# Staggering the row merges of gathered expert units against their high and low halves

## The chip, the core and the metric

One core of one Trainium2 chip runs the kernel. The metric is device time in microseconds, the median of several executions. Engines are named as in the profile: PE is TensorE (PEld its weight loads), DVE is VectorE, ACT is ScalarE, POOL is GpSimd, SP is SyncE, which issues most DMAs here (SPq is its queue).

## What is computed

Three stages in a row over 4608 tokens of width 512: linear attention with an RMS norm, a dense layer with a maximum of three products, and a top-2 mixture of eight experts. The change lies in the last stage alone:

```python
noisy_logits = x @ w_gate + np.log1p(np.exp(x @ w_noise)) * noise
top2 = np.argpartition(-noisy_logits, 2, axis=1)[:, :2]
# top2_w: softmax over the two chosen logits
for e in range(8):
    for k in range(2):
        mask = top2[:, k] == e
        h = np.maximum(x[mask] @ w1[e], 0.0)        # 512 -> 1024
        out[mask] += top2_w[mask, k, None] * (h @ w2[e])   # 1024 -> 512
```

## The kernel before

**Numbers in two halves.** Matrix products run on float32 values split into a high half (rounded to the fast matmul type) and a low half (the rest). A product is three passes: high by high, high by low, low by high. The split of a weight block is `split` (L292 on ScalarE for the high half, L293 on VectorE for the low half).

**Rows by expert.** While the dense layer runs in nine chunks of 512 tokens, each token's row is scattered to a table `Xg` in device memory, sorted by expert. A row is stored as two planes of 16 bits. The mixture then works on **units**: a unit is one, two or four blocks of 128 rows of one expert, with that expert's weights. The order is fixed: units 0, 1 and 2 have four blocks, and from unit 3 on a four-block unit (odd numbers) is followed by a small one (even numbers): units 4, 6 and 8 have one block, units 10 to 24 have two. Five spare one-block units stand behind branches that are not taken here.

**A unit's steps.** A unit has eight steps, f = 0 to 7, one for each 128 columns of the hidden width. Step f does the first product of f (`G1`, L1068; for a one-block unit L1082, at even f only, two f at once), then ScalarE's Relu (L1072 or L1085) and VectorE's low half (L1073). For a one-block unit the result is transposed two steps later (`hT1`, L1093, with L1094 and L1095 for its halves h). The second products (`G2`, L1130) of a step wait in a list `fifo`, sorted by unit and f, until a step number given with them: for larger units two steps later; for a one-block unit two steps after `hT1` for its first f and three for its second. At f = 7 ScalarE scales the output row out of its PSUM bank (L1135) and POOL adds it to the output by an indirect DMA (L1104). Four PSUM banks serve the second products in turn (`abank`), four the first products and transposes (`hbank`).

**Preparing the next unit.** During unit u the rows of unit u + 1 are made ready by `utrans`, block by block. The two 16-bit planes come by a transposing DMA into RA or RB (`load_rows`, L755, with weights and tokens of the rows at L756). A block is then *merged*: two copies (L790) interleave the planes into one of two buffers MG, one copy on VectorE and the other on ScalarE, or both on VectorE where `tight` is set (while a one-block unit runs). Then ScalarE makes the high half (L793) and VectorE the low half (L794) in the unit's x, which all first products of unit u + 1 read. Before, one call does all four instructions of a block. For u > 1 blocks 0 and 1 are called in step 2 and blocks 2 and 3 in step 4; for u < 2 in steps 3 and 5.

**Queues.** Every engine runs its instructions in the order in which this code writes them; a waiting instruction holds all behind it. SP's queue holds the register loads for a unit's expert and start row (`regs_of`, L741 and L742), the row DMAs and the weight loads (`load_pair`, L144) into three staging buffers. A load is written when the second split of the block three before it is. Before, unit u asks for the rows of unit u + 2 in step 4 if unit u + 1 has four blocks, otherwise in step 2. The table `SPL` says how many weight splits are written in each step:

```python
    SPL = {4: (2,) * 8, 2: (1,) * 8, 1: (0, 0, 0, 0, 0, 0, 1, 1)}
```

A split is left out when its weight slot may still be read or its load is not written yet. Within a step the order is: first product, transposes (`turn`), second products (`flush`), a piece of the table of units (steps 0 to 9 only), then `utrans` and `splits`.

Of the kernel before, what the change touches and what calls it, by code (L numbers as in the profile page):

```python
# [12 lines left out]
U16 = mybir.dt.uint16  # L13
# [72 lines left out]
def body(tc, A, dbg=None):  # L86
# [695 lines left out]

    def utrans(u, i, tight=False):
        s = slice(i * 128, (i + 1) * 128)
        pl = rplanes(u)
        g = MG[mgn[0] % 2]
        mgn[0] += 1
        h = g.bitcast(U16).rearrange("p (k t z) -> p k t z", k=4, z=2)
        for q in range(2):
            (ACT.copy if q and not tight else DVE.tensor_copy)(h[:, :, :, q], pl[:, 4 * q:4 * q + 4, s])  # L790
        t = g.rearrange("p (k t) -> p k t", k=4)
        x = xTu[u % 2]
        ACT.activation(x[0][:, :, s], t, AF.Copy)  # L793
        DVE.tensor_tensor(x[1][:, :, s], t, x[0][:, :, s].bitcast(F), op=OP.subtract)  # L794
        if i == units[u] - 1:
            m = units[u]
            DVE.tensor_copy(wid[u % 3][:, 0:m], gt[u % 3][:, 0:m, 0])
            DVE.tensor_copy(idt[u % 3][:, 0:m], gt[u % 3][:, 0:m, 1])


    def splits(k):
# [68 lines left out]
    def window(c):  # L870
# [8 lines left out]
        def trans(i):  # L879
            xtrans(c + 1, i) if nx else utrans(0, i)  # L880

# [7 lines left out]
        for i in range(4):  # L889
# [10 lines left out]
            if not nx:  # L900
                if i < 2:
                    trans(2 * i)
                    trans(2 * i + 1)
                if i == 1:
                    load_rows(1)
                splits(1)
# [181 lines left out]
    def hT1(u, f, hr):  # L1088
# [7 lines left out]
        fifo.append((step[0] + 2, u, f, h, 0))  # L1096
        fifo.append((step[0] + 3, u, f + 1, h, 128))

# [73 lines left out]
    tg = table()  # L1172
    SPL = {4: (2,) * 8, 2: (1,) * 8, 1: (0, 0, 0, 0, 0, 0, 1, 1)}

    def unit(u):
        mn = units[u + 1] if u + 1 < len(units) else 0
        for f in range(8):
            G1(u, f)
            turn(step[0])
            flush(step[0])  # L1180
            for _ in range(pump.get(step[0], 0)):
                next(tg, None)
            if u < 2:
                if f in (3, 5):
                    for i in range(2):
                        utrans(u + 1, f - 3 + i)
                if u == 1 and f == 7:
                    load_rows(3)
            splits(SPL[units[u]][f])
            if u > 1:  # L1190
                if f in (2, 4):
                    for i in range(f - 2, min(f, mn)):
                        utrans(u + 1, i, units[u] == 1)
                if f == (4 if mn == 4 else 2) and u + 2 < len(units):
                    regs_of(u + 2)
                    load_rows(u + 2)
                    loads()
            step[0] += 1
# [61 lines left out]
```

## Time and profile before

| what | value |
|---|---|
| median of 3 runs | 1556.95 us (1556.66 to 1558.84) |
| the profiled execution's own time | 1555.75 us |
| its span, first to last instruction | 1554.0 us |
| PE busy | 1515.0 us, 97% |
| DVE, ACT, POOL busy | 51%, 42%, 14% |
| mean granted clock of PE | 0.991 of full |
| mixture stage | from some 702 us to the end |

Busy shares are over the whole span. The chain of waits says which engine's work ended last at each moment; the list of waits says who stood for whom. A matmul's shown duration overlaps with the next one's, so the time of a product is read from the chain, which gives the twelve matmuls of a product as one piece.

### The profile page before, as it was taken

The page shows a single profiled execution, that of the slowest core. Times are in us where ns is not written, and L with a number is a line of the kernel's source. Part 1 is how long each engine was busy: PE and PEld are TensorE (multiplying, and loading weights), DVE is VectorE, ACT ScalarE, POOL GpSimd, SP SyncE. Part 2 cuts the span into 40 slices and gives each one's busy share as a digit, 9 for nine tenths or more (in the row PEclk, how much of TensorE's full clock was granted, in tenths as well). Part 3 has the DMA queues.
Part 4 walks back from the last instruction along what each step waited for, and adds up shares of the span by engine and source line. Part 5 has one row for each costly group of instructions (what it writes and reads, how often), then busy time and mean ns, then how long its engine had stood idle before and what let it go on. Part 6 is the DMA issues. An engine that isn't in the chain of part 4 may idle for free.

```text
span 1554.0 us, 23767 instructions
## 1 busy us (share of the span) xinstructions
PE 1515.0 (97%) x9564; PEld 1306.2 (84%) x9564; DVE 792.4 (51%) x1573; ACT 646.0 (42%) x1036; POOL 221.4 (14%) x326
## 2 busy tenths in 40 slices
PE   5999999999999999999999999999999999999997
PEld 4789989898989898888888787778888888888886
DVE  5985534343534343457454456465463554535443
ACT  3544322231313131343454445455464554645544
POOL 0000211111020202024211102101021010211102
PEclk8999999999999999999999999999999999999999
DMA  7322643031212101063676477766695666858554
GB/s 295 134 82 90 254 197 116 29 117 42 103 56 89 56 29 56 1 191 123 205 196 143 109 223 184 169 209 171 162 222 132 196 161 165 202 150 217 148 157 77
DMA packets 132292, 219.82 MB, mean 141 GB/s; under 512 B 96464, under 2 KB 96720, under 8 KB 114640
## 3 DMA queue, kind: packets, MB, share of 16 engines
q1 hardware_dynamic: 112320, 166.50, 34.0%
q0 software_dynamic: 19856, 51.73, 14.7%
q8 instruction: 77, 1.26, 0.3%
q14 instruction: 39, 0.32, 0.1%
HBM read 146.30 MB, written 51.72 MB: 127 GB/s over the span
## 4 chain that ended last, share of the span: by engine, by line
PE 92%; DVE 3%; ACT 2%; DMA 1%; issue 1%; POOL 1%; SPq 0%; POOLq 0%; ACTq 0%
PE bank L311 28%; PE bank L1068 24%; PE bank L1130 24%; PE bank L357 10%; PE bank L192 1%; PE bank L214 1%; PE bank L273 1%; DVE mg L790 1%; ACT B L793 1%; DMA pad<-kvr 1%; PE bank L1082 1%; DMA G<-kv 0%; POOL Xg L427 0%; DVE xlo L794 0%; PE bank L501 0%
## 5 line engine op out<-in xcount | busy, mean ns | idle before, releaser
L311 PE MATMUL bank<-B,W 128*128 128x512 f32 (+1 forms) x2160 | 455.5, 372 | 6.6 <-ACT W L482 4.2
L311 PEld LDWEIGHTS bank<-B,W 128*128 128x128 f32 x2160 | 377.6, 190 | 75.8 <-ACT W L482 4.9
L1130 PE MATMUL bank<-W,B 128*128 128x512 f32 x1728 | 423.3, 392 | 2.0 <-ACT xn L1135 1.9
L1130 PEld LDWEIGHTS bank<-W,B 128*128 128x128 f32 x1728 | 321.2, 189 | 67.0 <-ACT xn L1135 2.3
L1068 PE MATMUL bank<-B,W 128*128 128x512 f32 (+1 forms) x1728 | 355.0, 343 | 6.9 <-ACT B L793 6.9
L1068 PEld LDWEIGHTS bank<-B,W 128*128 128x128 f32 x1728 | 280.9, 190 | 51.1 <-ACT B L793 8.7
L293 DVE TENSOR_TENSOR W<-G,W 128x1024 fp32r<-128x1024 f32 x200 | 242.1, 1223 | 120.2 <-ACT W L292 119.6
L292 ACT ACTIVATE W<-G 128x1024 fp32r<-128x1024 f32 x200 | 207.6, 1055 | 53.3 <-PE bank L1130 39.8
L1073 DVE SCALAR_TENSOR_TENSOR B<-bank,B 128x512 fp32r<-128x512 f32 (+1 forms) x176 | 103.8, 592 | 207.1 <-ACT B L1072 206.6
L1072 ACT ACTIVATE B<-bank 128x512 fp32r<-128x512 f32 (+1 forms) x176 | 90.4, 516 | 266.7 <-PE bank L1068 265.5
L357 PE MATMUL bank<-W,B 128*128 128x256 f32 (+1 forms) x1296 | 164.0, 286 | 0.0
L357 PEld LDWEIGHTS bank<-W,B 128*128 128x128 f32 x1296 | 160.2, 188 | 1.1
L427 POOL DMA_INDIRECT Xg<-RA,si x72 | 72.1, 1001 | 522.1 <-issue 378.1
L329 DVE TENSOR_TENSOR hm<-hm,bank 128x512 f32<-128x512 f32 (+1 forms) x106 | 69.5, 656 | 132.3 <-PE bank L311 125.6
L315 ACT ACTIVATE B<-hm 128x512 fp32r<-128x512 f32 (+1 forms) x53 | 32.2, 607 | 184.7 <-DVE hm L329 184.7
L1068 PE MATMUL bank<-xlo,W 128*128 128x512 f32 x384 | 103.2, 391 | 0.0
L1104 POOL DMA_INDIRECT out<-xn,idt x37 | 61.3, 1655 | 275.3 <-ACT xn L1135 268.3
L1068 PEld LDWEIGHTS bank<-xlo,W 128*128 128x128 f32 x384 | 72.3, 188 | 15.1
L793 ACT ACTIVATE B<-mg 128x512 fp32r<-128x512 f32 x76 | 48.0, 632 | 84.4 <-DVE mg L790 84.3
L1104 POOL DMA_INDIRECT out<-x2T,idt x19 | 30.4, 1602 | 266.0 <-ACT x2T L1135 263.6
L364 ACT COPY RA<-bank 128x256 uint16<-128x256 uint16 x72 | 25.7, 372 | 88.0 <-DVE RA L364 72.7
L794 DVE TENSOR_TENSOR xlo<-mg,B 128x512 fp32r<-128x512 f32 x49 | 34.0, 694 | 36.7 <-ACT B L793 36.7
(184 smaller groups left out, 1010.4 us busy)
## 6 DMA issues: line engine op xcount, KB each, us to landing
G<-mw SPq DMA_DIRECT2D x100, 1024.0 KB, 5.1
G<-w1s SPq DMA_DIRECT2D x12, 1024.0 KB, 4.9
out<-pad POOLq DMA_DIRECT2D x1, 9472.0 KB
kv<-kv SPq DMA_DIRECT2D x8, 1024.0 KB, 7.2
G<-kv SPq DMA_DIRECT2D x8, 1024.0 KB, 9.7
RB<-qT SPq DMA_DIRECT2D x8, 1024.0 KB, 5.1
G<-kvr SPq DMA_DIRECT2D x7, 256.0 KB, 9.8
Xg<-RA,si POOLq DMA_INDIRECT x72, 2.7
```

Source lines behind the costliest of these rows:

```text
L292: ACT.activation(w[:, 0:1024], src, AF.Copy)
L293: DVE.tensor_tensor(w[:, 1024:2048], src, w[:, 0:1024].bitcast(F), op=OP.subtract)
L311: PE.matmul(bank[:, 0:t1 - t0], w_in(g)[:, a, k, s], x[b][:, k, t0:t1], start=n == 0 and k == 0, stop=n == 2 and k == 3)
L329: DVE.tensor_tensor(hm, hm, bank, op=OP.max)
L357: PE.matmul(x2b[i][z][:, 0:hi - lo], h[:, a, s], w[:, b, lo:hi], start=f == 0 and n == 0, stop=f == 5 and n == 2)
L427: i = POOL.indirect_dma_start(out=Xg, out_offset=bass.IndirectOffsetOnAxis(ap=idx, axis=0), in_=src, in_offset=None)
L793: ACT.activation(x[0][:, :, s], t, AF.Copy)
L1068: PE.matmul(bank[:, 0:n], w[:, a, k, s], x[b][:, k, 0:n], start=z == 0, stop=z == 11)
L1072: ACT.activation(h[:, 0, 0:n], bank[:, 0:n], AF.Relu)
L1073: DVE.scalar_tensor_tensor(h[:, 1, 0:n], bank[:, 0:n], 0.0, h[:, 0, 0:n].bitcast(F), op0=OP.max, op1=OP.subtract)
L1104: d = POOL.indirect_dma_start(out=A["out"], out_offset=bass.IndirectOffsetOnAxis(ap=idt[u % 3][:, i:i + 1], axis=0), in_=y, in_offset=None ...
L1130: PE.matmul(obank[i], h[:, a, s], w[:, b, ff % 2, :], start=ff == 0 and n == 0, stop=ff == 7 and n == 2)
```

## The change

`utrans` is cut in two: `merge` writes a block's two copies, `merged` its high and low half. In step n of the preparation block n is merged and block n - 1 gets its halves. The preparation starts in step 2 of a unit (step 1 in unit 0 and in one-block units, step 3 in unit 1). While a one-block unit runs, VectorE does both copies for blocks 0 and 2, and for blocks 1 and 3 ScalarE does one of them. Rows of unit u + 2 are asked for in step 0. Both second products of a pair of a one-block unit wait two steps. Four-block units split one weight half instead of two in their first two steps.

```diff
--- before.py
+++ after.py
@@ -780,15 +780,16 @@
 
     xTu = [xT]
 
-    def utrans(u, i, tight=False):
+    def merge(u, i, k=1):
         s = slice(i * 128, (i + 1) * 128)
         pl = rplanes(u)
-        g = MG[mgn[0] % 2]
-        mgn[0] += 1
-        h = g.bitcast(U16).rearrange("p (k t z) -> p k t z", k=4, z=2)
+        h = MG[i % 2].bitcast(U16).rearrange("p (k t z) -> p k t z", k=4, z=2)
         for q in range(2):
-            (ACT.copy if q and not tight else DVE.tensor_copy)(h[:, :, :, q], pl[:, 4 * q:4 * q + 4, s])
-        t = g.rearrange("p (k t) -> p k t", k=4)
+            (ACT.copy if q and k else DVE.tensor_copy)(h[:, :, :, q], pl[:, 4 * q:4 * q + 4, s])
+
+    def merged(u, i):
+        s = slice(i * 128, (i + 1) * 128)
+        t = MG[i % 2].rearrange("p (k t) -> p k t", k=4)
         x = xTu[u % 2]
         ACT.activation(x[0][:, :, s], t, AF.Copy)
         DVE.tensor_tensor(x[1][:, :, s], t, x[0][:, :, s].bitcast(F), op=OP.subtract)
@@ -797,6 +798,11 @@
             DVE.tensor_copy(wid[u % 3][:, 0:m], gt[u % 3][:, 0:m, 0])
             DVE.tensor_copy(idt[u % 3][:, 0:m], gt[u % 3][:, 0:m, 1])
 
+    def utrans(u, i, n):
+        if i < n:
+            merge(u, i, i % 2 if u > 2 and units[u - 1] == 1 else 1)
+        if 0 < i <= n:
+            merged(u, i - 1)
 
     def splits(k):
         for _ in range(k):
@@ -877,7 +883,7 @@
                 norm(c + 1, i + 2)
 
         def trans(i):
-            xtrans(c + 1, i) if nx else utrans(0, i)
+            xtrans(c + 1, i)
 
         if c == 0:
             for i in (2, 3):
@@ -899,8 +905,8 @@
                 fill(1)
             if not nx:
                 if i < 2:
-                    trans(2 * i)
-                    trans(2 * i + 1)
+                    for r in range(3 * i, 3 * i + 3 - i):
+                        utrans(0, r, 4)
                 if i == 1:
                     load_rows(1)
                 splits(1)
@@ -1094,7 +1100,7 @@
         ACT.activation(h[:, 0, 0:256], TR[:, 0:256], AF.Copy)
         DVE.tensor_tensor(h[:, 1, 0:256], TR[:, 0:256], h[:, 0, 0:256].bitcast(F), op=OP.subtract)
         fifo.append((step[0] + 2, u, f, h, 0))
-        fifo.append((step[0] + 3, u, f + 1, h, 128))
+        fifo.append((step[0] + 2, u, f + 1, h, 128))
 
     held = []
     added = {-1: zeroed}
@@ -1170,7 +1176,7 @@
 
     pump = {0: 1, 2: 1, 3: 2, 4: 2, 5: 2, 6: 2, 8: 1, 9: 1}
     tg = table()
-    SPL = {4: (2,) * 8, 2: (1,) * 8, 1: (0, 0, 0, 0, 0, 0, 1, 1)}
+    SPL = {4: (1, 1, 2, 2, 2, 2, 2, 2), 2: (1,) * 8, 1: (0, 0, 0, 0, 0, 0, 1, 1)}
 
     def unit(u):
         mn = units[u + 1] if u + 1 < len(units) else 0
@@ -1180,21 +1186,16 @@
             flush(step[0])
             for _ in range(pump.get(step[0], 0)):
                 next(tg, None)
-            if u < 2:
-                if f in (3, 5):
-                    for i in range(2):
-                        utrans(u + 1, f - 3 + i)
-                if u == 1 and f == 7:
-                    load_rows(3)
+            if u > 1 and f == 0 and u + 2 < len(units):
+                regs_of(u + 2)
+                load_rows(u + 2)
+                loads()
+            f0 = 3 if u == 1 else 1 if u == 0 or units[u] == 1 else 2
+            if mn and f >= f0:
+                utrans(u + 1, f - f0, mn)
+            if u == 1 and f == 7:
+                load_rows(3)
             splits(SPL[units[u]][f])
-            if u > 1:
-                if f in (2, 4):
-                    for i in range(f - 2, min(f, mn)):
-                        utrans(u + 1, i, units[u] == 1)
-                if f == (4 if mn == 4 else 2) and u + 2 < len(units):
-                    regs_of(u + 2)
-                    load_rows(u + 2)
-                    loads()
             step[0] += 1
 
     def drain():
```

What this moves, at three places. First, VectorE's queue in unit 4, the first one-block unit, from its first h to the last low half of unit 5's rows (h is L1095 before and L1101 now, RB holds the planes, mg is a buffer MG, xlo the low half of x). Before:

```order
L1095 TENSOR_TENSOR h_0_6243<-bank_108,h_0_6243 128x256
L790 COPY mg_281<-RB 128x512 x2
L794 TENSOR_TENSOR xlo<-mg_281,B_87 128x4x128
L790 COPY mg_280<-RB 128x512 x2
L794 TENSOR_TENSOR xlo<-mg_280,B_87 128x4x128
L1095 TENSOR_TENSOR h_1_6244<-bank_106,h_1_6244 128x256
L790 COPY mg_281<-RB 128x512 x2
L794 TENSOR_TENSOR xlo<-mg_281,B_87 128x4x128
L790 COPY mg_280<-RB 128x512 x2
L794 TENSOR_TENSOR xlo<-mg_280,B_87 128x4x128
```

Now:

```order
L788 COPY mg_280<-RB 128x512 x2
L1101 TENSOR_TENSOR h_0_6243<-bank_108,h_0_6243 128x256
L788 COPY mg_281<-RB 128x512
L795 TENSOR_TENSOR xlo<-mg_280,B_87 128x4x128
L788 COPY mg_280<-RB 128x512 x2
L795 TENSOR_TENSOR xlo<-mg_281,B_87 128x4x128
L1101 TENSOR_TENSOR h_1_6244<-bank_106,h_1_6244 128x256
L788 COPY mg_281<-RB 128x512
L795 TENSOR_TENSOR xlo<-mg_280,B_87 128x4x128
L795 TENSOR_TENSOR xlo<-mg_281,B_87 128x4x128
```

The copies of block 0 stand ahead of h, one copy each of blocks 1 and 3 is gone (ScalarE has it), and each low half stands behind the next block's copies.

Second, TensorE's queue at the beginning of unit 5 (xn is unit 4's h before its transposes, h its two halves, W_75 and W_77 its second weights, B_87 and xlo unit 5's x, B_86 unit 5's h). Before:

```order
L1093 MATMUL bank_106<-cst,xn_93 128x128 x2
L1130 MATMUL bank_110<-W_75,h_0_6243 128x512 x3
L1068 MATMUL bank_107<-B_87,W_78 128x512 x4
L1068 MATMUL bank_107<-xlo,W_78 128x512 x4
L1068 MATMUL bank_107<-B_87,W_78 128x512 x4
L1130 MATMUL bank_110<-W_75,h_0_6243 128x512 x3
L1068 MATMUL bank_108<-B_87,W_80 128x512 x4
L1068 MATMUL bank_108<-xlo,W_80 128x512 x4
L1068 MATMUL bank_108<-B_87,W_80 128x512 x4
L1130 MATMUL bank_110<-W_77,h_1_6244 128x512 x3
L1068 MATMUL bank_105<-B_87,W_80 128x512 x4
L1068 MATMUL bank_105<-xlo,W_80 128x512 x4
```

Now:

```order
L1099 MATMUL bank_106<-cst,xn_93 128x128 x2
L1136 MATMUL bank_110<-W_75,h_0_6243 128x512 x6
L1074 MATMUL bank_107<-B_87,W_78 128x512 x4
L1074 MATMUL bank_107<-xlo,W_78 128x512 x4
L1074 MATMUL bank_107<-B_87,W_78 128x512 x4
L1074 MATMUL bank_108<-B_87,W_80 128x512 x4
L1074 MATMUL bank_108<-xlo,W_80 128x512 x4
L1074 MATMUL bank_108<-B_87,W_80 128x512 x4
L1136 MATMUL bank_110<-W_77,h_1_6244 128x512 x6
L1136 MATMUL bank_111<-W_79,B_86 128x512 x3
L1136 MATMUL bank_112<-W_79,B_86 128x512 x3
L1136 MATMUL bank_109<-W_79,B_86 128x512 x3
```

Unit 4's second products stand in groups of six, and unit 5's own second products (B_86) begin one first product earlier.

Third, SP's queue in unit 5 (tabi is the table of units, mw the weights in device memory), as a difference:

```order
 L144 ISA
 L144 DMA G_83<-mw 128x2048
-L144 ISA
-L144 DMA G_84<-mw 128x2048
-L144 ISA
-L144 DMA G_82<-mw 128x2048
-L144 ISA
-L144 DMA G_83<-mw 128x2048
 L741 TENSOR_LOAD tabi
 L741 ISA x2
```

The register loads, and the row DMAs behind them, stand three weight loads earlier; these follow them now.

## Rows read from the trace of the kernel before

**Rows 1.** The page: busy time by engine, and the chain that ended last.

```profile
PE 1515.0 (97%) x9564; PEld 1306.2 (84%) x9564; DVE 792.4 (51%) x1573; ACT 646.0 (42%) x1036; POOL 221.4 (14%) x326
...
PE 92%; DVE 3%; ACT 2%; DMA 1%; issue 1%; POOL 1%; SPq 0%; POOLq 0%; ACTq 0%
```

**Rows 2.** Waits of TensorE, 690 to 1554 us: total us, times, longest us.

```profile
PE bank L1068 <- ACT B L793: 6.9, 4, 2.3
PE bank L1130 <- ACT xn L1135: 1.9, 1, 1.9
```

**Rows 3.** Chain in order of time, 845 to 1130 us: start us, us, what.

```profile
878.68 1.45 PE bank L1082 x12
...
889.30 3.06 PE bank L1068 x12
892.36 0.22 PE bank L1093 x2
...
905.62 3.69 PE bank L1130 x15
...
1027.57 5.30 PE bank L1130 x15
...
1054.64 1.43 PE bank L1068 x12
...
1082.64 1.36 PE bank L1130 x6
...
1093.52 2.72 PE bank L1068 x12
```

**Rows 4.** Timeline, 866 to 912 us: start, us, instruction, [idle before it, releaser].

```profile
880.42 0.38 ACT L1094 ACTIVATE h<-bank 128x256 fp32r<-128x256 f32 x1
...
880.84 0.42 DVE L1095 TENSOR_TENSOR h<-bank,h 128x256 fp32r<-128x256 f32 x1 [6.71 <-ACT h L1094]
881.18 0.79 DVE L790 COPY mg<-RB 128x512 uint16<-128x512 uint16 x2
...
882.00 0.63 ACT L793 ACTIVATE B<-mg 128x512 fp32r<-128x512 f32 x1 [1.20 <-DVE mg L790]
...
882.66 0.69 DVE L794 TENSOR_TENSOR xlo<-mg,B 128x512 fp32r<-128x512 f32 x1 [0.70 <-ACT B L793]
```

**Rows 5.** Stretches behind the second and third crossing: busy us by engine, PEclk.

```profile
949.00:955.00 6.00, 6.00 (x22) 4.77 (x21) 4.38 (x9) 4.08 (x7) 0.00 (x0) 0.72 0.25 67
...
1010.00:1016.00 6.00, 6.00 (x28) 4.87 (x27) 5.49 (x10) 4.60 (x6) 0.00 (x0) 1.00 0.26 75
```

**Rows 6.** Timeline, 1022 to 1028 us.

```profile
1026.36 0.58 ACT L1072 ACTIVATE B<-bank 128x512 fp32r<-128x512 f32 x1
...
1026.84 0.68 ACT L1135 ACTIVATE xn<-bank,wid 128x512 f32<-128x512 f32 x1
...
1027.57 0.73 PE L1130 MATMUL bank<-W,B 128*128 128x512 f32 x2 [1.88 <-ACT xn L1135]
```

**Rows 7.** Groups by line, whole span: count, busy us, mean ns, idle before.

```profile
L790 ACT COPY mg<-RB 128x512 uint16<-128x512 uint16 x41 | 31.6, 771 | 0.0
```

**Rows 8.** Timeline of the last two-block unit, 1530 to 1554 us.

```profile
1531.12 0.69 DVE L794 TENSOR_TENSOR xlo<-mg,B 128x512 fp32r<-128x512 f32 x1 [0.76 <-ACT B L793]
...
1532.34 1.22 DVE L293 TENSOR_TENSOR W<-G,W 128x1024 fp32r<-128x1024 f32 x1
```

**Rows 9.** SP's issues in order of time, 870 to 925 us: start, us, instruction.

```profile
893.16 10.61 SPq L144 DMA_DIRECT2D G<-mw  x4
905.08 5.50 SPq L755 DMA_TRANSPOSE RB<-Xg  x1
...
911.56 11.35 SPq L144 DMA_DIRECT2D G<-mw  x3
```

**Rows 10.** DMA issues of the page: count, KB each, median us to landing.

```profile
G<-mw SPq DMA_DIRECT2D x100, 1024.0 KB, 5.1
...
G<-kv SPq DMA_DIRECT2D x8, 1024.0 KB, 9.7
```

## Prediction

> **What bounds the kernel now.** I read the page first: TensorE is busy 97% of the span, and the chain of waits that ended last is 92% TensorE [rows 1]. So a change of ScalarE's and VectorE's order can only give back time in which TensorE stands or runs at its lower clock. Next I asked who TensorE waits for from 690 us on, the stretch that the change touches. Besides three short ones, only five idle times are listed: four in front of a first product (L1068), 6.9 us, all for ScalarE's high half of the transposed rows (L793), and one of 1.9 us in front of a second product (L1130), for ScalarE's output row (L1135) [rows 2]. Last I took the chain in order of time around the three single-block units 4, 6 and 8 [rows 3] and the engines' own rows there [rows 4, 6]. The reader should see that TensorE loses time at three crossings (from a single-block unit to the four-block unit behind it) and hardly anywhere else.
>
> What happens at a crossing is in [rows 4]. VectorE sits 6.71 us with nothing to do, because the next instruction in its queue is the low half of the single unit's own h (L1095), behind ScalarE's h at 880.42. Only then come the next unit's four blocks, one after the other. Each is two copies on VectorE (0.79), high half on ScalarE (0.63), low half on VectorE (0.69), and in each ScalarE waits some 1.20 us for the copies and VectorE 0.70 us for the high half. TensorE starts the next unit at 889.30.
>
> **Term A: the three crossings.** The second first-product of unit 4 ends at 878.68 + 1.45 = 880.13 [rows 3]. Until the next unit TensorE has to do three pairs of transposes (0.22 each), two single-block first products (1.45) and twice six second products (1.36): 0.66 + 2.90 + 2.72 = 6.28 us. It takes until 889.30, which is 9.17, so 2.89 us are lost. The crossings behind units 6 and 8 repeat these rows within 0.02 us. The first product behind one takes 3.06 where twelve such matmuls otherwise take 2.72, 0.34 for the restart [rows 3]. Together 3 x (2.89 + 0.34) = 9.69 us.
>
> How much of it goes? In the new order VectorE does both copies of block 0 in the 6.71 us that were empty. After ScalarE's h its queue is: h 0.42, one copy 0.4 (half of 0.79), low 0.69, two copies 0.79, low 0.69, h 0.42, one copy 0.4, low 0.69, low 0.69 [rows 4], 5.2 us if it never waits. I walked both queues against each other. ScalarE does h 0.38, its new copy 0.77 [rows 7], high half 0 0.63: done at 882.2, so VectorE, there at 881.7, waits 0.5 us. Low 0, the copies of block 2 and low 1 end at 884.4. Only then is block 3's buffer free for ScalarE's copy (0.77, to 885.1). High 2 ends at 885.8, high 3 at 886.4, low 2 at 886.5, low 3 at 887.2. TensorE would arrive at 880.13 + 6.28 = 886.4 and wants the low halves four matmuls later (0.9 us), at 887.3. That is just in time, with no reserve, so I leave 0.2 us at each crossing: **9.69 - 0.6 = 9.1 us**. Bounds: 9.69 if nothing stays; if one wait of ScalarE for copies (1.20) stays at each crossing, 9.69 - 3.6 = 6.1.
>
> **Term B: the clock behind the second crossing.** Between 949 and 955 us the granted clock is 0.72 on average: part of the stretch at 1.2 GHz, the rest at 2.4. Behind the third crossing, after the same idle time, it is 1.00 [rows 5]. A share of 0.28 of these 6 us, **1.7 us**, goes if TensorE does not stand before it. The other bound is 0: the drop comes anyway.
>
> **Term C: the wait inside unit 9.** TensorE stops 1.88 us until 1027.57 [rows 6]: the fourth group of unit 9's second products needs the PSUM bank that unit 8's output row still holds. ScalarE reaches that row (L1135) only at 1026.84, because two copies, two high halves and their waits for VectorE stand in its queue in front of it. The next fifteen matmuls take 5.30 us, where 15 x 2.72 / 12 = 3.40 is normal [rows 3]: 1.90 more. In units 5 and 7 the same place costs 3.69 - 3.40 = 0.29 each. Total 1.88 + 1.90 + 0.58 = 4.36. The change puts both last second products of a small unit into step 2, and ScalarE's output row straight behind that step's Relu. The bank is wanted six plus nine matmuls after step 2's first product ends, 1.36 + 9 x 0.227 = 3.4 us. ScalarE needs 0.58 for the Relu, waits for the six (1.36), then needs 0.68 [rows 6]: done after about 2.1, 1.3 to spare. So I take all of it: **4.4 us**. Lower bound: a short stop stays and with it the slow matmuls, 5.30 - 3.69 = 1.6, which leaves 2.75.
>
> The Trainium skill, TensorE: Matmul & The Clock Gate, section "What's actually happening", says that the ramp is run-variable. By that rule the same stand costs a drop in one run and none in another, as the crossings here do among themselves, and the clock's 1.7 + 1.9 us in B and C would be luck of this execution: the sum would be 11.6 instead of 15.2.
>
> **What is added, and what hides it.** Six copies go from VectorE to ScalarE, 771 ns each there [rows 7]: they lie in the crossings and are in the walk above. One split fewer in each of the first two steps of a four-block unit costs nothing: fourteen splits there and two in a single-block unit are the sixteen weight halves that both use, so the lead does not shrink; where a two-block unit follows there are 22 for 16. Were that cover gone, a first product would wait for VectorE's part of a split, 1.22 us [rows 8]. Rows asked for at step 0 stand on SP's queue ahead of the unit's weight loads. From the transpose's issue (905.08) to the next load's (911.56) it holds them 6.5 us [rows 9]; it does so today, two to four steps later, and TensorE does not wait behind it. Unit 1 now ends its merges in its last step: ScalarE's Relu and high half, then VectorE's low half, end some 2.0 us after that step's first product (0.58 + 0.63 + 0.69), while TensorE has twelve second products (2.7 us) before it needs the high half. Covered. The earlier rows of unit 0 and of the last chunk lie under matmuls that do not pause.
>
> **Sum.** 9.1 + 1.7 + 4.4 = 15.2 us. The profiled execution took 1555.75, which gives 1540.55; the median of the three runs shown, 1556.95, lies 1.2 above it, so I forecast **1541.7**.
>
> **Rivals.**
> 1. *The wait only shrinks.* The walk of term A has no reserve. If 1.20 us stays at each crossing, and a drop of the clock with it (B = 0), the gain is 6.1 + 4.4 = 10.5: 1546.5. For it: high 3 ready at 886.4, wanted at 886.4. Against: VectorE starts with a block done. Chance 0.10.
> 2. *The clock's share is no gain.* A drop follows some smaller stand as it followed the second crossing but not the third: 15.2 - 3.6 = 11.6, 1545.3. Against: after 690 us both places with slow matmuls come behind a stand of about 2 us. This is what the rule on the ramp above would do here. Chance 0.06.
> 3. *VectorE becomes the bound in two-block units.* There a middle step has 0.42 + 0.4 + 0.69 + 1.22 = 2.73 us for VectorE [rows 4, 8] and 1.43 + 1.36 = 2.79 for TensorE [rows 3]. Each wait for a high half (0.76 [rows 8]) is lateness; three such steps make 2.3 us, and in the seven two-block units with a four-block unit behind them 16 us, which eats the gain: 1557.7. Against: an h is used two steps, 5.6 us, later, and the rival decides only if lateness passes that. Chance 0.04.
> 4. *Slower: weights come late behind the rows.* After a single-block unit four load issues fit in 10.61 us, about 3.4 apart, and with three buffers a load has 10.2 us from issue to its split. Held 6.5 us [rows 9], and landing in 9.7 as 1024 KB loads in company do, where those of weights take 5.1 [rows 10], it is 6.0 us late. Splits lead TensorE by two pairs, 6.8 us; with one pair of lead instead, 2.6 us of wait at each of the ten requests for four-block rows cost 26 us: 10.8 slower, 1567.8. It decides when the lead falls under 6.0 us. Against: the same request stands in the same queue today without a wait of TensorE. Chance 0.04.
>
> The Trainium skill, DMA: Bandwidth & Descriptors, section "Issuing engines are not separate DMA queues", bears on rival 4: all transfers interleave on the same 16 engines whoever starts them. Rows asked for at step 0 would meet the previous unit's output rows, which POOL adds in step 1; by that rule a landing lengthens towards the 9.7 us above.
>
> **How the numbers follow.** My forecast has 0.76, the rivals 0.10, 0.06, 0.04 and 0.04. The range reaches from 1539.5 (every bound at its best, 15.7, and the scatter of runs, whose lowest is 0.3 under the median, with some room) to 1547.5, which takes in rivals 1 and 2; outside lie 3 and 4. About 0.2% (3.1 us) is what a measurement can tell from no change: faster 0.92, same 0.04, slower 0.04.
>
> **What would show it.** Right: from 690 us on TensorE's waits for the high half shrink from 6.9 us to below 1, none for an output row is left, no stretch before the tail has a clock of 0.72, and two copies stand in VectorE's 6.71 us before h. Wrong in A: an idle time over 1 us at the three crossings, released by the high half. Wrong in C: TensorE waiting for an output row in units 5, 7 or 9. Rival 2 would show as a low clock without a stand before it, rival 3 as TensorE waiting for VectorE's h in a two-block unit, rival 4 as ScalarE's split waiting for the weight load and TensorE for the split.

## The result, and the profile after

| | before | changed |
|---|---|---|
| median, same chip | 1556.93 us (1556.66 to 1558.84) | 1540.04 us (1538.49 to 1540.29, 4 runs) |
| the profiled execution's own time | 1555.75 us | 1540.13 us |
| its span | 1554.0 us | 1538.4 us |
| TensorE's waits after 690 us, before the tail | [rows 2] | none listed |

The changed kernel is faster: ratio 0.9888, interval 0.9872 to 0.9903, 16.9 us. I had forecast 1541.7; the time came out 1.7 us lower, on the lower end of my range (the ratio, which goes by all executions, times the median shown ahead is 1539.5). From the changed kernel on, the lines behind the new functions carry numbers 6 higher: first product L1074, second L1136, output row L1141, h L1100 and L1101. The two copies of a merge are L788, the high half L794, the low half L795.

The page of the changed kernel, as [rows 1]: busy time by engine, and the chain that ended last.

```profile
PE 1508.5 (98%) x9564; PEld 1304.2 (85%) x9564; DVE 789.7 (51%) x1567; ACT 644.8 (42%) x1042; POOL 222.3 (14%) x326
...
PE 96%; DMA 1%; DVE 1%; ACT 1%; issue 0%; POOL 0%; SPq 0%; POOLq 0%; DVEq 0%; ACTq 0%
```

TensorE's share of the chain rose from 92% to 96%, its busy time fell by 6.5 us. The rest of the gain is time in which it stood. Asked for TensorE's waits from 690 us on, the trace of the changed kernel gives an empty list, where [rows 2] had 8.8 us.

The granted clock shows the same. Two stretches of the changed kernel (busy us by engine, then PEclk), the first at the times of [rows 5], the second where the clock fell in the kernel before, behind the stop of [rows 6]:

```profile
949.00:955.00 6.00, 6.00 (x28) 4.96 (x27) 2.97 (x4) 4.06 (x6) 1.18 (x2) 1.00 1.20 223
...
1028.00:1034.00 6.00, 6.00 (x28) 4.96 (x27) 3.61 (x4) 2.49 (x3) 0.00 (x0) 1.00 0.51 178
```

Both are at 1.00. In the profile before, TensorE's clock fell twice between 690 us and the tail, in 949 to 955 us [rows 5] and in 1028 to 1034 us, both 0.72; the second stretch there:

```profile
1028.00:1034.00 6.00, 6.00 (x21) 4.80 (x20) 2.36 (x2) 1.41 (x2) 1.40 (x2) 0.72 1.23 289
```

Where the time came from is read off the chain of both kernels, at the places where the same matmuls stand. First the changed kernel's chain in order of time (start us, us, what):

```profile
743.24 2.72 PE bank L1136 x12
...
885.91 2.73 PE bank L1074 x12
...
895.72 4.08 PE bank L1136 x18
...
905.24 2.72 PE bank L1074 x12
...
960.98 2.72 PE bank L1074 x12
...
1016.72 2.72 PE bank L1074 x12
...
1524.93 2.08 PE bank L1136 x9
```

Then, of the kernel before, three pieces of the same view that did not stand above:

```profile
740.69 3.01 PE bank L1068 x12
...
966.45 3.69 PE bank L1130 x15
...
1541.12 2.08 PE bank L1130 x9
```

| place (what has just ended) | before | after | gained here | forecast here |
|---|---|---|---|---|
| unit 1's first product | 743.70 | 743.24 | 0.46 | not priced |
| unit 5's fourth group | 909.31 | 905.24 | 3.61 | 3.32 |
| unit 7's | 970.14 | 960.98 | 5.09 | 5.02 |
| unit 9's | 1032.87 | 1016.72 | 6.99 | 6.81 |
| last second products | 1543.20 | 1527.01 | 0.04 | 0 |
| end of the span | 1554.0 | 1538.4 | -0.59 | 0 |

(Before's places are ends: 740.69 + 3.01, 905.62 + 3.69 and 1027.57 + 5.30 of [rows 3], 966.45 + 3.69, 1541.12 + 2.08. The changed kernel's rows start where these end, the last one ends at 1524.93 + 2.08. The forecast column is the prediction's own terms by place: each crossing 3.23 less 0.2, with 0.29, with 0.29 and the clock's 1.7, and with 1.88 + 1.90.) So all of the gain comes where it was forecast, but for half a microsecond in front of unit 1. Between unit 9 and the end, 500 us with all units from 10 on, nothing is gained or lost. The last row is scatter: from the start of the last matmul to the end of the span it took 9.1 us in the profile of before, 9.7 in that of the changed kernel, and 9.3, 9.5 and 9.8 in late_rows, all_vector and old_first below.

How a crossing looks now is in the timeline of the changed kernel at the first one (start, us, instruction, [idle before it, releaser]), to be laid beside [rows 4]:

```profile
873.58 0.79 DVE L788 COPY mg<-RB 128x512 uint16<-128x512 uint16 x2
...
880.23 0.79 ACT L788 COPY mg<-RB 128x512 uint16<-128x512 uint16 x1
880.37 0.42 DVE L1101 TENSOR_TENSOR h<-bank,h 128x256 fp32r<-128x256 f32 x1 [6.00 <-ACT h L1100]
...
880.87 1.15 ACT L794 ACTIVATE B<-mg 128x512 fp32r<-128x512 f32 x2
...
883.76 0.79 ACT L788 COPY mg<-RB 128x512 uint16<-128x512 uint16 x1 [1.20 <-DVE xlo L795]
...
884.41 1.14 ACT L794 ACTIVATE B<-mg 128x512 fp32r<-128x512 f32 x2
885.06 1.30 DVE L795 TENSOR_TENSOR xlo<-mg,B 128x512 fp32r<-128x512 f32 x2 [0.63 <-ACT B L794]
...
885.75 1.08 PE L1074 MATMUL bank<-B,W 128*128 128x512 f32 x4
...
886.67 1.07 PE L1074 MATMUL bank<-xlo,W 128*128 128x512 f32 x4
```

The first row is block 0's merge, 6.8 us ahead of h, in what was VectorE's idle time. ScalarE's copies for blocks 1 and 3 are at 880.23 and 883.76, the four high halves come in two pairs. The last high half ends at 884.41 + 1.14 = 885.55; TensorE starts the unit at 885.75. The low halves end at 886.36; their first matmul is at 886.67. Some 0.2 and 0.3 us are left over, and the other two crossings repeat these rows. ScalarE's list of waits from 690 to 1520 us tells the same. In the kernel before, two of its lines (line waited for: total us, times, longest) were:

```profile
ACT B L793 <- DVE mg L790: 83.0, 73, 9.8
...
ACT W L292 <- DMA G<-mw: 10.1, 2, 8.8
```

The high half waited for its merge 73 times, 83.0 us in all, and now once, 1.5 us; the same two lines in the changed kernel:

```profile
ACT W L292 <- DMA G<-mw: 10.9, 2, 9.5
...
ACT B L794 <- DVE mg L788: 1.5, 1, 1.5
```

That is not time gained by itself: ScalarE's wait for the first products (L1072, now L1078) grew by as much, from 256.8 to 337.9 us. What counts is the order at the crossings. The split's wait for a weight load, the mark of rival 4, is as long as it was: 10.1 and 10.9 us, two times.

### The profile page after: what moved, and what is told of

Read it like the earlier page. It is cut to its first block, busy times and chain, and to the rows that moved or that the text cites. A ratio compares the mean times of both kernels' runs of the same rounds, so it can differ in the third digit from the quotient of the medians.

```text
span 1538.4 us, 23747 instructions
## 1 busy us (share of the span) xinstructions
PE 1508.5 (98%) x9564; PEld 1304.2 (85%) x9564; DVE 789.7 (51%) x1567; ACT 644.8 (42%) x1042; POOL 222.3 (14%) x326
## 4 chain that ended last, share of the span: by engine, by line
PE 96%; DMA 1%; DVE 1%; ACT 1%; issue 0%; POOL 0%; SPq 0%; POOLq 0%; DVEq 0%; ACTq 0%
PE bank L311 28%; PE bank L1136 27%; PE bank L1074 26%; PE bank L357 10%; PE bank L192 1%; PE bank L1088 1%; PE bank L214 1%; PE bank L273 1%; DMA pad<-kvr 1%; DMA G<-kv 0%; DMA G<-w1s 0%; PE bank L501 0%; DVE RA L478 0%; DVE B L282 0%; PE bank L493 0%
## 5 line engine op out<-in xcount | busy, mean ns | idle before, releaser
L1136 PE MATMUL bank<-W,B 128*128 128x512 f32 x1728 | 421.3, 390 | 0.0
L1136 PEld LDWEIGHTS bank<-W,B 128*128 128x128 f32 x1728 | 320.2, 188 | 63.4
L1074 PE MATMUL bank<-B,W 128*128 128x512 f32 (+1 forms) x1728 | 353.0, 342 | 0.0
L1074 PEld LDWEIGHTS bank<-B,W 128*128 128x128 f32 x1728 | 280.5, 189 | 42.5
L1078 ACT ACTIVATE B<-bank 128x512 fp32r<-128x512 f32 (+1 forms) x176 | 91.5, 520 | 340.8 <-PE bank L1074 340.8
L1074 PE MATMUL bank<-xlo,W 128*128 128x512 f32 x384 | 102.6, 389 | 0.0
L1074 PEld LDWEIGHTS bank<-xlo,W 128*128 128x128 f32 x384 | 72.1, 188 | 15.0
L327 ACT ACTIVATE hm<-bank 128x512 f32<-128x512 f32 (+1 forms) x53 | 30.4, 573 | 53.8 <-PE bank L311 41.5
L1110 POOL DMA_INDIRECT out<-hm,idt x19 | 33.0, 1735 | 134.2 <-ACT hm L1141 130.4
```

Source lines behind the costliest of these rows:

```text
L1074: PE.matmul(bank[:, 0:n], w[:, a, k, s], x[b][:, k, 0:n], start=z == 0, stop=z == 11)
L1078: ACT.activation(h[:, 0, 0:n], bank[:, 0:n], AF.Relu)
L1110: d = POOL.indirect_dma_start(out=A["out"], out_offset=bass.IndirectOffsetOnAxis(ap=idt[u % 3][:, i:i + 1], axis=0), in_=y, in_offset=None ...
L1136: PE.matmul(obank[i], h[:, a, s], w[:, b, ff % 2, :], start=ff == 0 and n == 0, stop=ff == 7 and n == 2)
```

## The experiments

Eleven runs were made, and two levels of time occur. On the chip of the first eight kernels of the table (the second chip below) the kernel before takes 1570 to 1571 us; on that of the last three it takes 1557, as in the first measurement (both called the first chip below, for their level). A kernel is compared only with the runs of the kernel before that were made beside it, and where an expectation names a time of the first chip, its distance from the kernel before is what can be compared. Besides the medians I use the time from the 5,200th matmul, in the last chunk of the dense layer, to the start of the last one. It leaves out the start and the tail, in which the chips and the executions differ. It is 890.8 us in the profile of before and **874.6** in that of the changed kernel.

| label | what is kept of the change | us | ratio to its own before | 5,200th to last matmul |
|---|---|---|---|---|
| stagger_only | staggering alone | 1549.57 | 0.9866 (0.985 to 0.9883) | 875.5 |
| no_pair | all but the pairing | 1549.55 | 0.987 (0.9854 to 0.9887) | 874.7 |
| pair_only | pairing alone | 1566.36 | 0.9971 (0.9961 to 0.9982) | 892.9 |
| bunched | all but the staggering | 1564.35 | 0.9959 (0.9945 to 0.9974) | 889.6 |
| after_again | the changed kernel | 1548.99 | 0.9862 (0.9841 to 0.9883) | 874.7 |
| before_again | the kernel before, one execution | 1569.26 | | 895.9 |
| start_two | all, small units prepared one step later | 1553.56 | 0.9896 (0.9873 to 0.992) | 878.4 |
| even_splits | all but the moved splits | 1547.33 | 0.9861 (0.9837 to 0.9885) | 874.8 |
| old_first | all, units 1 and 2 prepared as before | 1539.7 | 0.9892 (0.9876 to 0.9909) | 875.5 |
| late_rows | all but the early request of rows | 1539.28 | 0.9884 (0.9867 to 0.99) | 874.7 |
| all_vector | all, both copies on VectorE in one-block units | 1540.72 | 0.9894 (0.9878 to 0.9911) | 874.6 |

### Which edit removes which wait

My theory had two parts: the staggering removes the stand at the crossings, the pairing removes the wait in unit 9. The rival: one of the two does it all, or the earlier rows do. Four kernels take the change apart.

**stagger_only** keeps `merge`, `merged` and their steps, so the earlier start and ScalarE's copies too, and puts back rows (behind the splits again), splits and fifo:

```diff
-        fifo.append((step[0] + 2, u, f + 1, h, 128))
+        fifo.append((step[0] + 3, u, f + 1, h, 128))
...
-    SPL = {4: (1, 1, 2, 2, 2, 2, 2, 2), 2: (1,) * 8, 1: (0, 0, 0, 0, 0, 0, 1, 1)}
+    SPL = {4: (2,) * 8, 2: (1,) * 8, 1: (0, 0, 0, 0, 0, 0, 1, 1)}
...
-            if u > 1 and f == 0 and u + 2 < len(units):
+            if u > 1 and f == (4 if mn == 4 else 2) and u + 2 < len(units):
```

> Only the staggered merges are kept: rows are asked for at the old steps, four-block units split two halves in every step, and the second products of one-block units wait two and three steps as before. Theory (the crossings are lost by the order of the merges alone): the three crossings and the clock behind them are gone, 9.7 + 1.7 us, and the stop in unit 9 too, because the two high halves no longer stand in front of the output row: 1540 to 1542, at most 0.3 us of wait left in front of a second product. Rival (the pairing does term C): the stop of 1.9 us and its slow matmuls stay, 1543 to 1546. Rival (rows or splits carry the gain): 1550 or more.

It took 1549.57 against 1571.21. This is all that TensorE waits for from 690 us to its tail:

```profile
PE bank L1136 <- issue: 0.3, 1, 0.3
```

Neither the crossings' wait nor the one for the output row is left. Staggering alone has the gain, all but the 0.8 us (875.5 to 874.7) that it is slower between the same matmuls.

**no_pair** is the changed kernel with the first line of that diff alone.

> The changed kernel without the pairing. Theory: within 0.5 us of the changed kernel, 1540.0 to 1540.5, since the staggering already frees ScalarE in front of the output row. Rival (the pairing is needed for term C): 1542 to 1545, with TensorE waiting for an output row in unit 9.

1549.55 against the same before, and no wait of TensorE after 690 us. So the pairing is not needed for the wait in unit 9: that step of my reasons is wrong, though its sum was right.

**pair_only** is the kernel before with the pairing alone:

```diff
-        fifo.append((step[0] + 3, u, f + 1, h, 128))
+        fifo.append((step[0] + 2, u, f + 1, h, 128))
```

> The kernel before with one edit: both second products of a one-block unit wait two steps. Theory: the three crossings stay (2.9 + 0.3 us each, with or without a drop of the clock), the stop in unit 9 goes: 4.4 us less than before, 1552.5, give or take 2 for the clock. Rival (TensorE's order helps the crossings): under 1548.

1566.36 against 1571.21, a ratio of 0.9971. TensorE's waits (line waited for: total, times, longest):

```profile
PE bank L1068 <- ACT B L793: 9.1, 4, 2.3
```

The line of the output row is gone here as well, while the crossings keep their 2.3 us. The gain, 4.9 us, is near the 4.4 of term C. Two stretches of this kernel, behind its stands in front of unit 1 and at the third crossing, have a low clock:

```profile
755.00:761.00 6.00, 6.00 (x21) 4.69 (x20) 4.17 (x11) 0.60 (x1) 0.00 (x0) 0.72 0.00 0
1024.00:1030.00 6.00, 6.00 (x21) 4.73 (x22) 4.22 (x8) 3.73 (x7) 0.00 (x0) 0.72 0.22 44
```

and its chain has the slow first product there, followed by a unit 9 without a stop (start us, us, what):

```profile
1023.86 4.62 PE bank L1068 x12
...
1035.53 4.08 PE bank L1130 x18
```

Eighteen matmuls in 4.08 us are 0.227 each: full speed. So each of the two edits removes the wait in unit 9 by itself. The causes overlap: the output row came late because merges and their waits stood in ScalarE's queue in front of it *and* because the last second products came a step later. To undo either is enough, and their gains don't add.

**bunched** keeps everything but the staggering; a block is merged and halved in one go again, in the old steps, and with both copies on VectorE while a one-block unit runs:

```diff
-            f0 = 3 if u == 1 else 1 if u == 0 or units[u] == 1 else 2
-            if mn and f >= f0:
-                utrans(u + 1, f - f0, mn)
+            f0 = 3 if u < 2 else 2
+            if f in (f0, f0 + 2):
+                for i in range(f - f0, min(f - f0 + 2, mn)):
+                    merge(u + 1, i, 0 if u > 1 and units[u] == 1 else 1)
+                    merged(u + 1, i)
```

> The changed kernel with one part undone: merges and halves of two blocks are written together in steps 2 and 4 (3 and 5 in units 0 and 1), all copies on VectorE while a one-block unit runs, as before. Pairing, earlier rows and the split table are kept. Theory: like the pairing alone, 1551 to 1554, with an idle time of some 2.3 us at each of the three crossings. Rival (the other three parts carry the gain): 1540 to 1543.

1564.35 against 1571.21. The crossings are back in full, three of 2.3 us and one of 1.04 in front of unit 1:

```profile
PE bank L1074 <- ACT B L794: 7.8, 4, 2.3
```

Early rows, pairing and moved splits together do nothing for them. The gain, 6.9 us, is above the 3 to 6 that I had expected and 2.0 above pair_only's; the stand in front of unit 1 is 1.04 us here and 2.34 there, and no run shows which of the other edits does that. Here the clock fell behind the second crossing and not behind the first:

```profile
902.00:908.00 6.00, 6.00 (x28) 4.89 (x28) 5.16 (x9) 3.70 (x5) 0.00 (x0) 1.00 0.27 70
961.00:967.00 6.00, 6.00 (x22) 4.73 (x21) 4.05 (x9) 3.60 (x5) 0.00 (x0) 0.72 0.31 78
```

### How much reserve there is, and who needs ScalarE's copies

**start_two** begins the preparation one step later while a one-block unit runs:

```diff
-            f0 = 3 if u == 1 else 1 if u == 0 or units[u] == 1 else 2
+            f0 = 3 if u == 1 else 1 if u == 0 else 2
```

> The changed kernel, but while a one-block unit runs the merges begin in step 2 instead of step 1, so block 0's copies stand behind the one-block unit's first h in VectorE's queue. Theory: one link more in the chain; each crossing stands 0.8 to 1.7 us plus 0.3 for the restart, 3.4 to 6 us above the changed kernel, and a low clock behind one of them adds up to 1.7. Rival (the interleaving alone is enough, the early start is not needed): equal to the changed kernel within 0.5 us.

3.7 us more between the same matmuls than in after_again (878.4 to 874.7), 4.6 in the medians. TensorE stands three times (total, times, longest):

```profile
PE bank L1074 <- ACT B L794: 2.9, 3, 1.0
```

In the timeline VectorE has its 6.71 us of idle time ahead of h again ([rows 4]), and the copies of block 0 come behind it, three copies in a row (the third is block 1's):

```profile
888.41 0.42 DVE L1101 TENSOR_TENSOR h<-bank,h 128x256 fp32r<-128x256 f32 x1 [6.71 <-ACT h L1100]
888.75 1.13 DVE L788 COPY mg<-RB 128x512 uint16<-128x512 uint16 x3
```

and the first product behind the stand takes the time of a restart, 3.03:

```profile
894.94 3.03 PE bank L1074 x12
```

Three times 0.95 + 0.31 are 3.8, about the difference. So of the 2.26 us for which TensorE stood at a crossing, the new order takes away 1.3 without the early start, and the last 0.95 go only when block 0 is merged ahead of h, with two copies that take 0.79 us. The other way round was not run: no kernel here starts early and still merges and halves a block in one go, so what the early start is worth alone stays open.

**all_vector** gives VectorE both copies of every block while a one-block unit runs:

```diff
-            merge(u, i, i % 2 if u > 2 and units[u - 1] == 1 else 1)
+            merge(u, i, 0 if u > 2 and units[u - 1] == 1 else 1)
```

> The changed kernel with both copies of every block on VectorE while a one-block unit runs, so none of the six copies moves to ScalarE. Theory from the same walk through the two queues: the last high half comes no later, since ScalarE no longer waits for a free merge buffer: within 0.5 us of the changed kernel, no idle time over 0.3 us at the crossings. Rival (VectorE is the last link and the six copies matter): 0.4 to 0.8 us of stand at each crossing, 2 to 4 us slower with the restarts.

1540.72 beside late_rows' 1539.28 on the same chip, whose intervals overlap; 874.6 between the same matmuls, as the changed kernel. No wait of TensorE after 690 us. At the first crossing (start, us, instruction):

```profile
885.11 1.50 DVE L795 TENSOR_TENSOR xlo<-mg,B 128x512 fp32r<-128x512 f32 x2
885.25 0.63 ACT L794 ACTIVATE B<-mg 128x512 fp32r<-128x512 f32 x1 [0.97 <-DVE mg L788]
...
886.42 1.07 PE L1074 MATMUL bank<-B,W 128*128 128x512 f32 x4
...
887.33 1.07 PE L1074 MATMUL bank<-xlo,W 128*128 128x512 f32 x4
```

The last high half ends at 885.88 and the unit starts at 886.42; the low halves end at 886.61, wanted at 887.33. There is more reserve than in the changed kernel (0.5 and 0.7 us instead of 0.2 and 0.3). Moving six copies to ScalarE was not needed, and takes reserve away: one copy takes ScalarE 0.79 us, as long as two take VectorE together.

### The parts without effect

**late_rows** asks for rows where the kernel before does:

```diff
-            if u > 1 and f == 0 and u + 2 < len(units):
+            if u > 1 and f == (4 if mn == 4 else 2) and u + 2 < len(units):
```

> The changed kernel with the rows asked for at the old steps (4 or 2). Theory: the request is a unit ahead of its use either way, so nothing changes: within 1 us of the changed kernel (1549 on the slower chip, 1540 on the first), no wait of TensorE in the mixture. Rival (early rows are needed for the merge in step 1): a wait of VectorE's first copy and 1 us or more at each crossing.

874.7 and 874.6 between the same matmuls: no difference. SP's queue of the changed kernel behind the first crossing (start, us, instruction) shows that the order did change:

```profile
889.47 0.33 SPq L144 DMA_DIRECT2D G<-mw  x1
891.09 5.07 SPq L755 DMA_TRANSPOSE RB<-Xg  x1
...
897.04 26.13 SPq L144 DMA_DIRECT2D G<-mw  x6
```

The rows (L755) now stand behind one weight load and ahead of six, and hold the queue 5 us, as the mechanism of rival 4 has it. No split and no matmul waits for it.

**even_splits** puts back two splits in each step of a four-block unit:

```diff
-    SPL = {4: (1, 1, 2, 2, 2, 2, 2, 2), 2: (1,) * 8, 1: (0, 0, 0, 0, 0, 0, 1, 1)}
+    SPL = {4: (2,) * 8, 2: (1,) * 8, 1: (0, 0, 0, 0, 0, 0, 1, 1)}
```

> The changed kernel with two splits in every step of a four-block unit, as before. Theory: no difference, within 0.5 us of the changed kernel, and no wait of TensorE. Rival (two more splits behind the crossing delay Relu and output row, so that TensorE stops in units 5, 7 and 9): 1 to 4 us slower.

874.8 beside 874.7: no difference, as the sum had it. Its median lies 1.7 us under after_again's, but the executions overlap (1546.45 to 1551.76 against 1547.11 to 1551.12).

### The place in front of unit 1, and the two chips

**after_again** and **before_again** are the two kernels unchanged, on the second chip.

> The changed kernel itself, on the chip of the experiments of this call. The chip of the first experiments lost 8 us between 160 and 176 us in every kernel and had a further stand of 2.3 us in front of unit 1's first product in kernels with the old order of merges. Theory: on such a chip the change is worth 20 to 22 us, since the staggering removes that stand too; on a chip like that of the first measurement 15 to 17. No idle time of TensorE after 690 us on either. Rival (the change's gain is fixed by the three crossings): 15 to 17 us on every chip.

> The kernel before with a profile on the same chip. Theory of the clock (a stand of 2.3 us is followed by a low clock in some executions and not in others): the three crossings and unit 9 show the same idle times as in the first profile, 2.26 us and 1.9, but the places with a low clock are others. Rival (the drop belongs to the second crossing and unit 9): low clock at exactly these two places again.

Here the change is worth more: 1569.94 to 1548.99, 21 us where the first chip gave 17. TensorE's waits of the kernel before on this chip (total, times, longest):

```profile
PE bank L1068 <- ACT B L793: 9.9, 4, 3.1
PE bank L1130 <- ACT xn L1135: 1.9, 1, 1.9
```

A fourth stand, 0.1 us on the first chip, is 3.10 us here, and the timeline says where: VectorE, still busy with the table of units (L1008 and other lines), merges the last blocks of unit 1 so late that TensorE stands in front of that unit (start, us, instruction):

```profile
748.34 0.52 DVE L1008 SCALAR_TENSOR_TENSOR G<-G,cst 128x288 f32<-128x288 f32 x1
...
748.77 0.45 DVE L790 COPY mg<-RB 128x512 uint16<-128x512 uint16 x1
...
752.00 1.22 PE L1068 MATMUL bank<-B,W 128*128 128x512 f32 x2 [3.10 <-ACT B L793]
```

The granted clock is low behind this stand, behind the third crossing and in unit 9. Around the second crossing, from 958 to 964 us on this chip, it is not (busy us by engine, PEclk):

```profile
750.00:756.00 6.00, 4.00 (x11) 3.23 (x12) 5.04 (x14) 2.20 (x4) 1.25 (x2) 0.72 0.23 89
...
958.00:964.00 6.00, 3.72 (x16) 2.63 (x16) 4.28 (x12) 3.41 (x6) 0.00 (x0) 1.00 0.51 74
...
1021.00:1027.00 6.00, 5.80 (x19) 4.62 (x20) 4.04 (x7) 3.73 (x8) 0.00 (x0) 0.72 0.15 26
...
1042.00:1048.00 6.00, 6.00 (x21) 4.77 (x20) 2.16 (x2) 0.71 (x1) 0.70 (x2) 0.72 1.21 300
```

Up to unit 1's end the changed kernel gains 5.6 us on this chip (50.7 us against 45.1 between the 5,600th and the 5,800th matmul), and 15.6 behind it. Both kernels are some 8 us slower on this chip in one early place (56.4 us against 48.5 between the 1,000th and the 1,500th matmul), where TensorE waits for nothing that the profile shows; in the changed kernel, from 150 to 185 us:

```profile
PE bank L214 <- issue: 2.7, 5, 1.1
PE bank L192 <- issue: 1.5, 2, 1.1
```

The first chip has neither line. Why the chips differ is open; I did not look for it, as both kernels show it.

**old_first** puts units 1 and 2 back to the old steps, two blocks at a time, and keeps the rest:

```diff
-            f0 = 3 if u == 1 else 1 if u == 0 or units[u] == 1 else 2
-            if mn and f >= f0:
-                utrans(u + 1, f - f0, mn)
+            if u < 2:
+                if f in (3, 5):
+                    for i in range(f - 3, f - 1):
+                        merge(u + 1, i)
+                        merged(u + 1, i)
+            elif mn and f >= (1 if units[u] == 1 else 2):
+                utrans(u + 1, f - (1 if units[u] == 1 else 2), mn)
```

> The changed kernel with the old order of merges in units 0 and 1 alone (two blocks in step 3, two in step 5); all later units staggered. On the chip of the other experiments (8 us lost at 160 to 176 us): theory (there the stand in front of unit 1's first product comes from the merges of blocks 2 and 3 standing behind the table's instructions in VectorE's queue): the stand is back, 2 to 3 us of idle time, 3 to 5 us above the changed kernel's 1549. On a chip like that of the first measurement: 0.5 us above 1540. Rival (that stand comes from something else in the old order): no idle time there, equal to the changed kernel.

One wait is back, in front of unit 1:

```profile
PE bank L1074 <- ACT B L794: 0.5, 1, 0.5
```

It makes 0.8 us between the same matmuls (875.5 to 874.7), 0.51 of stand and 0.3 of restart, too little to show in the medians of this chip. So the staggering pays at this place too, by 0.5 to 0.8 us here. On the other chip 5.6 us were gained there; old_first did not run on it.

## Why the prediction was right or wrong

**Right:** the bound (TensorE's stands are all that there is to gain), the sign, and the three places with their prices. 15.62 us came between the two profiled executions, where the sum had 15.2. Every sign named for "right" is there: no wait for the high half, none for an output row, no clock of 0.72, two copies in VectorE's idle 6.71 us (it is 6.00 now, the 0.79 of the copies taken out).

**Wrong:** the 1.2 us added from the profile to the median, and the sizes of two terms: the 0.2 us left at each crossing, and the stand in front of unit 1, priced at nothing.

**Term A, the crossings.** The links of the walk were right; its times were too long, and the step that failed is "just in time, with no reserve, so I leave 0.2 us at each crossing". Nothing stays. I had summed durations, while in these rows the next instruction of an engine starts before the one ahead has ended when its data is there: two high halves take 1.15, not 2 x 0.63, two low halves 1.30, not 2 x 0.69. The walk set the last high half at 886.4, which is 885.9 on the changed kernel's time axis (0.46 earlier since unit 1); it ended at 885.55. Rival 1 stood on the same missing reserve and fell with it. That cost the forecast 0.5 us (gained over the forecast at the three places of the table: 0.29, 0.07 and 0.18).

**Term B, the clock.** It came as priced, 1.7. Two falls behind the four stands of this execution are also the share that four executions show, 8 of 16 (last section); why it was these two, no run shows. Rival 2 fell: no profile has a low clock between 690 us and the tail without a stand of TensorE ahead of it, and the eight with no stand over 0.6 us there have none at all, whichever part of the change they lack.

**Term C, unit 9.** The size was right. The reason was half of it: pairing is sufficient, but staggering is too, and with it in place the pairing brings nothing.

**In front of unit 1.** "Covered" was right for the new order, but that step asked only whether the move costs something. [rows 2] list four waits for the high half and I priced three; the fourth, 0.1 us of stand and 0.3 of restart, gave 0.46, and on another chip 5.6.

**From the profile to the median.** The forecast added 1.2 us, because the profiled execution of before lay that far under its median. That is the largest step that failed: the changed kernel's profiled execution lies at its median (1540.13, 1540.04). 0.4 us more of gain (0.5 at the crossings and 0.5 in front of unit 1, less 0.6 in the tail) and this 1.2 (with the 0.1 between these two) are the 1.7 by which the time was missed. What made the 1.2 stays open. Executions of before can differ by how many stands the clock falls behind, at 1.7 us each, but only profiled executions show where it fell, and kernels without such a stand scatter as widely: the changed kernel between 1547.11 and 1551.12 us on the second chip, even_splits between 1546.45 and 1551.76. In the profiled executions of the eight kernels with no stand over 0.6 us after 690 us, the 1,000th matmul starts between 129.5 and 133.0 us, so a part of the scatter comes from the start of the kernel, with the change and without it. The 1.2 us lie within that scatter, and adding them to another kernel's sum had no ground. The range's lower end counted scatter as 0.3 us under a median, though the profiled execution itself lay 1.2 under its own, and was too high for that.

**Rival 3** (VectorE as the bound in two-block units): the trace has no wait for h there, and no time is lost between unit 9 and the end. **Rival 4** (weights late behind the rows): late_rows is the direct test, and shows no difference. Nor did the weights land later: on the changed kernel's page the median of their loads from issue to landing is 5.2 us, before 5.1 [rows 10], and not near the 9.7 that the prediction held possible.

No version is clearly faster than the changed kernel. From 690 us to the tail its trace lists no wait of TensorE; stagger_only gets all but 0.8 us of the gain with one edit instead of four.

## What to carry to other kernels

Where two engines hand a block back and forth (copy, high half, low half), write block n's first step ahead of block n - 1's last ones, and put the first block's into the idle time ahead of the instruction that the queue waits at: here the first without the second left 0.95 us of each stand. Find by single edits which part of a change carries it: here one of four did, and two edits each removed the same wait. Don't add the distance between one profiled execution and a median to the forecast for another kernel: here such a distance was no more than scatter, and the largest part of the miss.

## What the hardware showed that was not expected

TensorE's clock falls behind equal stands in one case and not in another. Four profiled executions (before, before_again, pair_only, bunched) have 16 stands of 1.88 to 3.10 us after 690 us; behind 8 of them the clock fell to half for a while, behind the other 8 it did not, and the same place (the second or the third crossing) is on either side in different executions. Each fall costs some 1.7 us: 0.28 of the 6 us of a stretch at a mean of 0.72. Behind six stands of 0.51 to 1.04 us (start_two, bunched, pair_only, old_first) it did not fall. The Trainium skill, TensorE: Matmul & The Clock Gate, section "What's actually happening", calls the ramp run-variable; the traces agree in that the place of a fall varies from execution to execution, while all falls between 690 us and the tail come behind a stand. So in these traces a stand of about 2 us cost 2 us, 0.3 for the restart and, in half of the cases, 1.7 more.
